# Lo parts that are loaded as weights start 112 bytes into their buffers

## The chip, the cores and the metric

The kernel runs on one core of a Trainium2 chip. TensorE multiplies matrices: an instruction loads a block of weights (128 x 128 here), and a matmul streams up to 512 columns through it into PSUM. VectorE (DVE), ScalarE (ACT) and GpSimd (POOL) do the elementwise work, and SyncE (SP) issues most transfers. The metric is the device time of one execution in microseconds; for the kernel before it is 877.3, the median of three runs.

## The reference

The input x has 2,048 rows of 448 floats. Two layers follow each other, with the same weights. Each is a linear-attention block and a feed-forward block, with a layer norm ahead of each:

```python
phi = lambda t: jnp.where(t > 0, t + 1, jnp.exp(t)) + 1e-6
pq, pk = phi(q), phi(k)                       # q, k, v = x @ wqkv, 16 heads of 28
kv = jnp.einsum("bhsd,bhse->bhde", pk, v)
z = jnp.einsum("bhsd->bhd", pk)
num = jnp.einsum("bhqd,bhde->bhqe", pq, kv)
den = jnp.einsum("bhqd,bhd->bhq", pq, z)[..., None] + 1e-6
o = num / den                                 # then @ wo
...
h = gelu(jnp.einsum("bsd,df->bsf", x, w1) + b1)    # 448 -> 1792
return jnp.einsum("bsf,fd->bsd", h, w2) + b2       # 1792 -> 448
...
x = x + A(layernorm(x)); x = x + B(layernorm(x))   # twice
```

Everything is float32.

## The kernel before

**Split operands.** TensorE takes a rounded float32 (`F32R`) at one column a cycle. To keep accuracy, each operand is split into a hi part, the rounded value, and a lo part, the rest. A product then takes three matmuls: hi by hi, hi by lo, lo by hi. Where only 64 of 448 rows are left over, hi and lo of these rows share one block and two matmuls do.

**Stages.** The 2,048 rows are 16 tiles of 128. For each layer, `phase1` walks over the 16 tiles: the normalized tile is transposed and split into `XH` and `XL`; `stage_k` and `stage_q` multiply it with the weights of k and q (lines 325 to 330, outputs `psk` and `psq`); `stage_g` multiplies the normalized tile itself, as weights, with phi(k) and adds all tiles up into four PSUM banks `G` (lines 526 to 538). `stage_s` makes its hi and lo parts `xnh` and `xnl`. A short stage in an order written out by hand (`ORDER`) then turns G and the weights of v and of the output into one matrix M (`kvp`, line 698, and `mp`, line 708, are plain float32 matmuls there).

Then the feed-forward part goes over four blocks of four tiles and, in each, over 14 steps of 128 of the 1,792 hidden columns. `mlp1` (lines 858 to 862, output `hp`) makes a step's hidden values: 11 matmuls of 512 columns, in which w1 is the weights and the tokens stream. ScalarE applies gelu (line 864) and copies the hi part `gh` (line 867), VectorE subtracts for the lo part `gl` (line 868). `mlp2` (lines 891 to 893, output `y`) has gelu's parts as weights and streams 448 columns of w2: for each of four tiles `gh` by `w2h`, `gh` by `w2l`, `gl` by `w2h`. The loop issues `mlp1` of step i + 1 ahead of `mlp2` of step i, so that gelu of a step has a whole `mlp1` to finish in. In the same steps, after a table of plans, the product of the next block's queries with M is done (`oc_mm`, lines 800 to 804, output `op`, with `qh` and `ql` as weights); for the first block of a layer `o_mm` does it (lines 789 to 791).

**Buffers.** `t512(tag, bufs, name, dt)` takes a tile of 128 x 512 floats, 2,048 bytes a partition, from a ring of `bufs` buffers per tag. The hi parts `xnh`, `gh` and the first block's `qh` use tag A, their lo parts tag B; other queries use E and F. All rings have two buffers here, and all slices that are loaded as weights are 128 columns, 512 bytes, apart. Two unread tiles named `space` (192 and 128 bytes) stand between the others; by the sizes of all tiles in the order of their allocation, the tiles that TensorE reads in its one-pass matmuls begin at multiples of 256 bytes. SBUF is filled nearly to its end.

**Tails.** For the first eight tiles of the first layer the transposition is done on TensorE. The last 64 columns of such a tile are copied twice into a 128 x 128 tile `tail` (line 413, ScalarE), which is transposed like the other three pieces (lines 257 and 264). `tail` has two buffers. `b2b` is the bias b2 on all partitions: one transfer fills it behind `phase1` of the first layer (line 1003), and `add_bias` (line 820) adds it on GpSimd in the feed-forward part.

The tile framework places the semaphores: a reader waits for the writer of what it reads, a writer for the readers of what it overwrites. Instructions run in the order of the program on each engine.

Of the kernel before, what the change touches and what calls it, by code (L numbers as in the profile page):

```python
# [9 lines left out]
F32 = mybir.dt.float32  # L10
F32R = mybir.dt.float32r
# [11 lines left out]
def linear_attn_mlp_kernel(  # L23
# [16 lines left out]
    F = w1.shape[1]  # L40
# [4 lines left out]
    G = 112  # L45
# [6 lines left out]
    work = ctx.enter_context(tc.tile_pool(name="work", bufs=2))  # L52
# [9 lines left out]
    def bank(tag, bufs, name):  # L62
        return psum.tile([128, 512], F32, name=name, tag=tag, bufs=bufs)
# [4 lines left out]
        bufs = NH if tag == "H" else bufs  # L68
        return work.tile([128, D], dt, name=name, tag=tag, bufs=bufs)

    def t512(tag, bufs, name, dt=F32):
        return work.tile([128, 512], dt, name=name, tag=tag, bufs=bufs)

    def f(ap):
        return ap.bitcast(F32)
# [82 lines left out]

    ones = consts.tile([128, 128], F32R, name="ones")
    one = t512("e", 3, "one")[:, :128]  # L160
    dve.memset(one, 1.0)
    dve.tensor_copy(ones, one)
# [23 lines left out]
    b2b = consts.tile([128, D], F32, name="b2b")  # L186
# [123 lines left out]
    def split_t(key, t, hi, lo, eng=dve):  # L310

        x = spreads[key, t // 2].rearrange("p (i c u n) -> p u c i n", i=4, c=4, n=32)[:, t % 2]
        h = hi.rearrange("p (c i n) -> p c i n", c=4, n=32)
        act.copy(h, x)  # L314
        eng.tensor_tensor(lo.rearrange("p (c i n) -> p c i n", c=4, n=32), x, f(h), op=OP.subtract)  # L315
# [85 lines left out]
    tails = {}  # L401
# [4 lines left out]
    def stage_n(l, t):  # L406

        xs, mv, rs = sts.pop((l, t))
        dve.tensor_scalar(xs, xs, mv[:, 0:1], rs, op0=OP.subtract, op1=OP.mult)
        xns[l, t] = xs  # L410
        if t < TURNED[l]:
            d = tails[l, t] = work.tile([128, 128], F32, name="tail", tag="tail", bufs=2)
            act.copy(d.rearrange("p (u n) -> p u n", u=2), xs[:, None, TL:].to_broadcast([128, 2, 64]))

    def stage_t(l, t):
# [24 lines left out]
    def stage_s(l, t):  # L440
        xn = xns.pop((l, t))
        h = t512("A", 2, "xnh", F32R)
        lo = t512("B", 2, "xnl", F32R)
        act.copy(h[:, :D], xn)  # L444
        pool.tensor_tensor(lo[:, :TL], xn[:, :TL], f(h[:, :TL]), op=OP.subtract)  # L445
        pool.tensor_tensor(h[:, D:], xn[:, TL:], f(h[:, TL:D]), op=OP.subtract)
        split[l, t] = (h, lo)
# [139 lines left out]
    def launch(za):  # L587
        for tok in LAUNCH.split():
            name, (j, *c) = tok.rstrip("0123456789"), [int(i) for i in tok if i.isdigit()]
            if name in ("ka", "qa"):  # L590
                split_hi(name[0], j, st_k if name == "ka" else st_q)
            elif name in ("kb", "qb"):
                split_lo(name[0], j, st_k if name == "kb" else st_q, pool if tok in ("kb1", "kb2", "qb0", "qb2") else dve)
            elif name in ("ha", "hb", "la", "lb"):
                split_half(("a", 0, 0), j, "ab".index(name[1]), "hi" if name[0] == "h" else "lo")
            elif name == "T":
                launch_t(j)
            elif name == "K":
                stage_k(0, j, c)
            elif name == "Q":  # L600
                stage_q(0, j, c)
            elif name == "kl":
                stage_kl(0, j, za)
            else:
                {"a": stage_a, "n": stage_n, "kp": stage_kphi, "kh": stage_kh, "s": stage_s}[name](0, j)

    def phase1(l, tr):
# [6 lines left out]
        for t in range(l == 0, NT):  # L614
            norm = NORM[l][t] if t < len(NORM[l]) else ()
            for tok in STEPS.get((l, t), STEP).split():
                if tok[1:].isdigit() and tok[0] in "anv":
                    {"a": stage_a, "n": stage_n, "v": stage_t}[tok[0]](l, int(tok[1:]))
                elif tok == "q1":
                    stage_qphi(1)  # L620
# [9 lines left out]
                elif tok == "n":  # L630
                    for u in norm:
                        stage_n(l, u)
# [109 lines left out]
    pqt, qs, pzs = {}, {}, {}  # L742
# [31 lines left out]
    def q_split(l, b, j):  # L774
        tp = tqs.pop((l, b, j))
        qh = t512("A", 2, "qh", F32R)[:G]
        ql = t512("B", 2, "ql", F32R)[:G]
        act.copy(qh, tp[:G])
        dve.tensor_sub(ql, tp[:G], f(qh))
        qs[l, b, j] = (qh, ql)  # L780
# [55 lines left out]
        turn(pqt.pop((l, b * 4 + j)), ("q", l, b), j)  # L836

    def q_part(l, b, j):
        qs[l, b, j] = t512("E", 2, "qh", F32R), t512("F", 2, "ql", F32R)
        split_t(("q", l, b), j, *qs[l, b, j])  # L840

    def m_prep(l, b, j):
# [9 lines left out]
    def mlp1(l, b, i):  # L852
        hp = bank("h", 2, "hp")
        s = slice(i * 128, (i + 1) * 128)
        x = blocks["m", l, b]
        o = hp.rearrange("p (t n) -> p t n", t=4)
        for c in range(3):
            pe.matmul(o, w1h[:, c, s], x.moving(x.hi, c), start=(c == 0), stop=False)  # L858
            pe.matmul(o, w1l[:, c, s], x.moving(x.hi, c), start=False, stop=False)  # L859
            pe.matmul(o, w1h[:, c, s], x.moving(x.lo, c), start=False, stop=False)  # L860
        pe.matmul(o, w1x[:, s], x.moving(x.hi, 3), start=False, stop=False)  # L861
        pe.matmul(o, w1x[:, s], x.moving(x.lo, 3), start=False, stop=True)  # L862
        g = t512("e", 3, "g")
        act.activation(g, hp, AF.Gelu_apprx_tanh, bias=b1s[:, i:i + 1])  # L864
        gh = t512("A", 2, "gh", F32R)
        gl = t512("B", 2, "gl", F32R)
        act.copy(gh, g)  # L867
        dve.tensor_sub(gl, g, f(gh))  # L868
        gs[i] = (gh, gl)
# [78 lines left out]
    def behind(l, b, i, tr):  # L948
        for tok in (PLAN_0, PLAN_1, PLAN)[min(b, 2)][i].split():
# [6 lines left out]
            if name == "ld":  # L956
                load_pq(l, k, j)
            elif name == "g":
                load_x(l, k * 4 + j)
            elif name == "z":  # L960
                q_z(l, k, j, tr)
            elif name == "p":
                q_prep(l, k, j, tr)
            elif name == "sq":
                store_sq(("q", l, k), j)
            elif name == "lq":
                spread(("q", l, k), j)
            elif name == "q":
                q_part(l, k, j)
            elif name == "o":  # L970
                oc_mm(l, k, j, tr)
                o_ln(l, k, j)
            elif name == "n":
                m_prep(l, k, j)
            elif name == "sx":
                store_sq(("m", l, k), j)
            elif name == "lx":
                spread(("m", l, k), j)
            elif name == "x":
                m_part(l, k, j)  # L980
# [12 lines left out]
    for l in range(LAYERS):  # L993
# [11 lines left out]
        def pre(j):  # L1005
# [9 lines left out]
            kv=lambda j: trans_kv(tr), mask=lambda j: trans_mask(tr), m=lambda j: trans_m(tr, j),  # L1015
            ms=lambda j: trans_ms(tr, j), qz=lambda j: q_z(l, 0, j, tr), qs=lambda j: q_scale(l, 0, j, tr),
            tq=lambda j: q_transpose(l, 0, j), qq=lambda j: q_split(l, 0, j), o=lambda j: o_mm(l, 0, j, tr),
            la=lambda j: o_ln(l, 0, j), lb=lambda j: o_n(l, 0, j), T=lambda j: m_transpose(l, 0, j),
            x=lambda j: m_split(l, 0, j), tu=lambda j: turn(xns.pop(("m", l, j)), ("m", l, 0), j),
            st=lambda j: store_sq(("m", l, 0), 0), sp=lambda j: spread(("m", l, 0), 0), pre=pre, b=biases)  # L1020
        for tok in ORDER.split():
            name, j = tok.rstrip("0123456789"), int("0" + tok.lstrip("abcdefghijklmnopqrstuvwxyzQTG"))
            getattr(tok_, name)(j)
        assert not fill and not qo
        table(AF.Gelu_apprx_tanh)
        q_z(l, 1, 0, tr)
        mlp1(l, 0, 0)
        trans_chunks(tr)
        for b in range(NB):
# [6 lines left out]
            for i in range(NF):  # L1036
                if i + 1 < NF:
                    mlp1(l, b, i + 1)
                elif nxt:
                    mlp1(l, b + 1, 0)  # L1040
                if l == 0 and b == 0 and i:
                    background(1, 1)
                if i == NF - 2 and not nxt and l + 1 < LAYERS:
                    table(AF.Exp)
                if 9 <= i < 13:
                    add_bias(l, b, i - 9)
                if nxt:
                    behind(l, b, i, tr)
                elif l + 1 < LAYERS:
                    if i == 2:  # L1050
                        split_kq("k", st_k)
                    if i == 5:
                        split_kq("q", st_q)
                    if i in (3, 4, 6, 7, 8):
                        t = (3, 4, 6, 7, 8).index(i)
                        stage_a(l + 1, t)
                        stage_n(l + 1, t)
                        stage_t(l + 1, t)
                        if t % 2:
                            stage_sp(l + 1, t)  # L1060
                    if 9 <= i < 13:
                        stage_x(l + 1, i - 9)
                mlp2(l, b, i, acc)
# [28 lines left out]
```

## Time and profile before

| | |
|---|---|
| median of three runs | 877.3 us (876.67 to 877.49) |
| span of the profiled execution, first to last instruction | 875.2 us |
| TensorE busy with matmuls | 870.1 us, 4182 records |
| weight loads busy | 772.0 us, 4182 records |
| VectorE, ScalarE, GpSimd busy | 491.2, 344.4, 221.1 us |
| matmuls y, three groups of 447 | 365 ns each by the record |
| matmuls hp, 512 columns | about 391 ns each by the record |

How to read it: a matmul's record lasts longer than the distance to the next one's start, because they are pipelined, and so the durations of matmuls overlap and their ends are modelled. PE is the row of matmuls, PEld that of the weight loads that run beside them. For the profiled execution the trace has the span; the time of the runs holds what lies around it as well. In the timeline a row is start, duration, engine, line, operation, output and inputs, and shapes, all times in us. In a group's row the numbers behind the bar are the busy time in us, the mean of one in ns, and the engine's idle time ahead of it with what ended it.

### The profile page before, as it was taken

The page shows a single profiled execution, that of the slowest core. Times are in us where ns is not written, and L with a number is a line of the kernel's source. Part 1 is how long each engine was busy: PE and PEld are TensorE (multiplying, and loading weights), DVE is VectorE, ACT ScalarE, POOL GpSimd, SP SyncE. Part 2 cuts the span into 40 slices and gives each one's busy share as a digit, 9 for nine tenths or more (in the row PEclk, how much of TensorE's full clock was granted, in tenths as well). Part 3 has the DMA queues.
Part 4 walks back from the last instruction along what each step waited for, and adds up shares of the span by engine and source line. Part 5 has one row for each costly group of instructions (what it writes and reads, how often), then busy time and mean ns, then how long its engine had stood idle before and what let it go on. Part 6 is the DMA issues. An engine that isn't in the chain of part 4 may idle for free.

```text
span 875.2 us, 11679 instructions
## 1 busy us (share of the span) xinstructions
PE 870.1 (99%) x4182; PEld 772.0 (88%) x4182; DVE 491.2 (56%) x958; ACT 344.4 (39%) x606; POOL 221.1 (25%) x250
## 2 busy tenths in 40 slices
PE   9999999999999999999999999999999999999998
PEld 8999988888888888888899998888888888888887
DVE  7878586658455443226477876864674483433112
ACT  6776635324323322333356665332233133223221
POOL 5566532235013112012222344110220140140000
PEclk9999999999999999999999999999999999999999
DMA  5474637633313402051145543352332423111001
GB/s 160 136 239 152 207 88 210 184 93 125 133 60 105 156 0 97 1 179 49 48 141 188 166 128 106 104 182 80 110 109 91 134 71 115 49 49 43 0 1 43
DMA packets 63642, 94.76 MB, mean 108 GB/s; under 512 B 8928, under 2 KB 58720, under 8 KB 63584
## 3 DMA queue, kind: packets, MB, share of 16 engines
q1 hardware_dynamic: 63408, 93.87, 33.5%
q8 instruction: 33, 0.54, 0.3%
q14 instruction: 25, 0.20, 0.1%
q10 hardware_dynamic: 176, 0.14, 0.0%
HBM read 56.17 MB, written 34.60 MB: 104 GB/s over the span
## 4 chain that ended last, share of the span: by engine, by line
PE 98%; DVE 0%; DMA 0%; POOL 0%; issue 0%; DVEq 0%; POOLq 0%
PE y L893 10%; PE y L892 10%; PE y L891 10%; PE hp L859 9%; PE hp L860 9%; PE hp L858 9%; PE hp L861 3%; PE hp L862 3%; PE psk L326 2%; PE psq L325 2%; PE psq L327 2%; PE psq L326 2%; PE psk L327 2%; PE psk L325 2%; PE G L534 2%; PE G L535 2%
## 5 line engine op out<-in xcount | busy, mean ns | idle before, releaser
L868 DVE TENSOR_TENSOR gl<-g,gh 128x512 fp32r<-128x512 f32 x112 | 82.6, 737 | 300.0 <-ACT gh L867 300.0
L864 ACT ACTIVATE g<-hp,b1s 128x512 f32<-128x512 f32 x112 | 77.1, 688 | 406.6 <-PE hp L862 401.8
L893 PE MATMUL y<-w2h,gl 128*128 128x448 f32 x447 | 163.3, 365 | 0.0
L892 PE MATMUL y<-w2l,gh 128*128 128x448 f32 x447 | 163.3, 365 | 0.0
L891 PE MATMUL y<-w2h,gh 128*128 128x448 f32 x447 | 163.3, 365 | 0.0
L859 PE MATMUL hp<-XH,w1l 128*128 128x512 f32 x336 | 131.5, 392 | 0.0
L858 PE MATMUL hp<-XH,w1h 128*128 128x512 f32 x336 | 131.2, 391 | 0.0
L860 PE MATMUL hp<-XL,w1h 128*128 128x512 f32 x336 | 131.2, 391 | 0.0
L214 POOL TENSOR_TENSOR brs<-bve,mhalf 128x1 f32<-128x1 f32 x64 | 39.4, 616 | 283.9 <-DVE bve L212 280.8
L891 PEld LDWEIGHTS y<-w2h,gh 128*128 128x128 f32 x447 | 84.0, 188 | 9.0
L892 PEld LDWEIGHTS y<-w2l,gh 128*128 128x128 f32 x447 | 84.0, 188 | 8.3
L893 PEld LDWEIGHTS y<-w2h,gl 128*128 128x128 f32 x447 | 84.0, 188 | 6.6
L860 PEld LDWEIGHTS hp<-XL,w1h 128*128 128x128 f32 x336 | 63.1, 188 | 14.1 <-issue 0.6
L859 PEld LDWEIGHTS hp<-XH,w1l 128*128 128x128 f32 x336 | 63.1, 188 | 11.3
L858 PEld LDWEIGHTS hp<-XH,w1h 128*128 128x128 f32 x336 | 63.1, 188 | 10.8
L867 ACT CAST gh<-g 128x512 fp32r<-128x512 f32 x112 | 69.7, 622 | 3.6
L751 POOL TENSOR_TENSOR pz<-pq,zb 128x448 f32<-128x448 f32 x32 | 36.6, 1147 | 82.6 <-DVE dn L757 65.9
L445 POOL TENSOR_TENSOR xnl<-x,xnh 128x384 fp32r<-128x384 f32 x32 | 35.0, 1092 | 72.6 <-ACT xnh L444 40.6
L315 DVE TENSOR_TENSOR XL<-sp,XH 128x512 fp32r<-128x512 f32 x50 | 44.4, 893 | 4.1 <-ACT XH L314 4.1
L862 PE MATMUL hp<-XL,w1x 128*128 128x512 f32 x112 | 43.6, 389 | 0.0
L861 PE MATMUL hp<-XH,w1x 128*128 128x512 f32 x112 | 43.6, 389 | 0.0
L820 POOL TENSOR_TENSOR x<-x,b2b 128x448 f32<-128x448 f32 x32 | 42.0, 1332 | 0.0
(169 smaller groups left out, 1566.8 us busy)
## 6 DMA issues: line engine op xcount, KB each, us to landing
x<-in_A_x_dram SPq DMA_DIRECT2D x32, 224.0 KB, 3.9
pq_d<-eq SPq DMA_DIRECT2D x32, 224.0 KB, 2.8
pq<-pq_d SPq DMA_DIRECT2D x32, 224.0 KB, 3.2
sq_m<-sq SPq DMA_DIRECT2D x14, 512.0 KB, 2.8
sp<-sq_m SPq DMA_DIRECT2D x56, 128.0 KB, 2.9
x<-x_d SPq DMA_DIRECT2D x32, 224.0 KB, 3.2
sq_a<-sq SPq DMA_DIRECT2D x12, 512.0 KB, 2.9
sp<-sq_a SPq DMA_DIRECT2D x48, 128.0 KB, 2.9
```

Of the source, the lines that this page charges most:

```text
L315: eng.tensor_tensor(lo.rearrange("p (c i n) -> p c i n", c=4, n=32), x, f(h), op=OP.subtract)
L858: pe.matmul(o, w1h[:, c, s], x.moving(x.hi, c), start=(c == 0), stop=False)
L859: pe.matmul(o, w1l[:, c, s], x.moving(x.hi, c), start=False, stop=False)
L860: pe.matmul(o, w1h[:, c, s], x.moving(x.lo, c), start=False, stop=False)
L861: pe.matmul(o, w1x[:, s], x.moving(x.hi, 3), start=False, stop=False)
L862: pe.matmul(o, w1x[:, s], x.moving(x.lo, 3), start=False, stop=True)
L864: act.activation(g, hp, AF.Gelu_apprx_tanh, bias=b1s[:, i:i + 1])
L867: act.copy(gh, g)
L868: dve.tensor_sub(gl, g, f(gh))
L891: pe.matmul(acc[j], gh[:, s], w2h[:, i], start=first, stop=False)
L892: pe.matmul(acc[j], gh[:, s], w2l[:, i], start=False, stop=False)
L893: pe.matmul(acc[j], gl[:, s], w2h[:, i], start=False, stop=stop)
```

## The change

Buffers of tags B and F become 576 floats long, 2,304 bytes, and `t512` gets a parameter `at`: the tile that it returns is the 512 floats from there. The lo parts that are loaded as weights (`xnl`, `ql` in both forms, `gl`) are taken at 28 floats, 112 bytes. Hi parts and all other tiles of these tags (`kl`, `zl`, `Ml`, `gt`) stay at 0. To make room for the four longer buffers (4 x 256 bytes), the two `tail` tiles (2 x 512 bytes) go: tails take turns in the first two 128-column parts of `b2b`, ahead of its transfer.

```diff
-    def t512(tag, bufs, name, dt=F32):
-        return work.tile([128, 512], dt, name=name, tag=tag, bufs=bufs)
+    APART = 28
+
+    def t512(tag, bufs, name, dt=F32, at=0):
+        n = 576 if tag in "BF" else 512
+        return work.tile([128, n], dt, name=name, tag=tag, bufs=bufs)[:, at:at + 512]
...
         if t < TURNED[l]:
-            d = tails[l, t] = work.tile([128, 128], F32, name="tail", tag="tail", bufs=2)
+            d = tails[l, t] = b2b[:, t % 2 * 128:][:, :128]
...
         h = t512("A", 2, "xnh", F32R)
-        lo = t512("B", 2, "xnl", F32R)
+        lo = t512("B", 2, "xnl", F32R, APART)
...
         qh = t512("A", 2, "qh", F32R)[:G]
-        ql = t512("B", 2, "ql", F32R)[:G]
+        ql = t512("B", 2, "ql", F32R, APART)[:G]
...
-        qs[l, b, j] = t512("E", 2, "qh", F32R), t512("F", 2, "ql", F32R)
+        qs[l, b, j] = t512("E", 2, "qh", F32R), t512("F", 2, "ql", F32R, APART)
...
         gh = t512("A", 2, "gh", F32R)
-        gl = t512("B", 2, "gl", F32R)
+        gl = t512("B", 2, "gl", F32R, APART)
```

## The prediction

> **What bounds the kernel.** I read the page first: the span, the busy shares, the granted clock and the chain.
>
> ```profile
> span 875.2 us, 11679 instructions
> PE 870.1 (99%) x4182; PEld 772.0 (88%) x4182; DVE 491.2 (56%) x958; ACT 344.4 (39%) x606; POOL 221.1 (25%) x250
> ...
> PEclk9999999999999999999999999999999999999999
> ...
> PE 98%; DVE 0%; DMA 0%; POOL 0%; issue 0%; DVEq 0%; POOLq 0%
> ```
>
> TensorE has work for 870.1 of 875.2 us at full granted clock, and the chain that ended last is 98% TensorE. So no other engine's work matters unless it makes TensorE wait, and the time is a count of matmuls times the distance from one start to the next. A busy share cannot show that distance, because matmuls overlap. I take it from the timeline of starts, in one step of the feed-forward part and in one stretch of the attention part of the first layer:
>
> ```profile
> 599.87 0.37 PE L891 MATMUL y<-w2h,gh 128*128 128x448 f32 x1
> ...
> 602.30 0.39 PE L858 MATMUL hp<-XH,w1h 128*128 128x512 f32 x1
> ...
> 603.00 0.40 PE L858 MATMUL hp<-XH,w1h 128*128 128x512 f32 x1
> ...
> 603.69 0.39 PE L858 MATMUL hp<-XH,w1h 128*128 128x512 f32 x1
> ...
> 604.82 0.36 PE L800 MATMUL op<-wq,qh 128*128 128x448 f32 x1
> ```
>
> ```profile
> 98.63 0.37 PE L534 MATMUL G<-kh,xnh 128*128 128x448 f32 x1
> ...
> 100.90 0.37 PE L325 MATMUL psq<-wq,XH 128*128 128x448 f32 x1
> ```
>
> ```profile
> 506.27 0.36 PE L534 MATMUL G<-kh,xnh 128*128 128x448 f32 x1
> ...
> 508.50 0.36 PE L325 MATMUL psk<-wk,XH 128*128 128x448 f32 x1
> ```
>
> Twelve y matmuls take 602.30 - 599.87 = 2.43 us, 202.5 ns each. Eleven G matmuls take 2.23 us late (202.7 ns each) and 2.27 us early (206.4 ns each): the same work, the same weights and columns, at two paces. With 512 columns, the first three behind y take 0.70 us (233 ns each) and the last five 1.13 us (226 ns each). So the distance has a part that depends on what came just before, not on the operation alone.
>
> What would the columns alone take? Two groups in plain float32 help, in which a record streams its columns twice:
>
> ```profile
> 108.19 3.31 PE L698 MATMUL kvp<-gt,stg 128*112 128x112 f32 x32
> 111.33 0.60 PE L769 MATMUL tq<-ident,pq 128*112 128x128 f32 x4
> ...
> 114.46 2.80 PE L708 MATMUL mp<-wot,kvm 112*112 112x448 f32 x7
> ...
> L708 PE MATMUL mp<-wot,kvm x16: 537/539/541, 114.5 to 546.9; 112*112 112x448 f32 x16
> ```
>
> The seven mp records last 2.80 us, the last one 0.54, so six distances make 2.26 us, 377 ns for two passes of 448 columns, 188 ns a pass, although each record has its own weight load. kvp gives (111.33 - 108.19) / 32 = 98 ns for two passes of 112, 49 ns a pass. Against 188 ns, a one-pass 448-column matmul loses 202.5 - 188 = 14.5 ns beside its weight load. (That a record is two passes I infer from these times.) This loss of about 14 ns, and its swing of 4 ns between the two paces, is all that a change of addresses can touch.
>
> **The change, part by part.** No instruction, semaphore or DMA is added or removed. Four things move.
>
> (1) The lo tiles used as weights begin 112 bytes into a longer buffer. The groups that load them:
>
> ```profile
> L893 PEld LDWEIGHTS y<-w2h,gl x447: 187/188/188, 143.3 to 870.4; 128*128 128x128 f32 x149
> ...
> L536 PEld LDWEIGHTS G<-kh,xnl x90: 187/188/189, 18.1 to 535.0; 128*128 128x128 f32 x90
> ...
> L528 PEld LDWEIGHTS G<-kh,xnl x6: 188/188/188, 94.7 to 525.1; 128*128 128x128 f32 x6
> ...
> L802 PEld LDWEIGHTS op<-wq,ql x72: 187/188/188, 168.0 to 762.0; 128*128 128x128 f32 x72
> L791 PEld LDWEIGHTS op<-Mh,ql x32: 187/188/188, 118.1 to 559.8; 112*128 112x128 f32 x32
> ...
> L804 PEld LDWEIGHTS op<-wq,ql x24: 187/188/188, 169.6 to 762.4; 128*128 128x128 f32 x24
> ```
>
> 447 + 90 + 6 + 72 + 32 + 24 = 671 loads (two more in the last output tile). Each takes 188 ns and runs under the matmul before it, and each is one of a group of about three 448-column matmuls, hi, hi, lo. What does the new start cost? By the sizes of the tiles in the order they are allocated, and with the program's unread spacers, every operand of these matmuls begins at a multiple of 256 bytes, so the trace holds no such start. The nearest rows are kvp and mp above: their weights are slices 448 bytes apart, thus at odd multiples of 64 bytes too, and each keeps one pace. But those have slack, 112 is no multiple of 64, and the one-pass matmuls have none. So the price is bounded from both sides:
> - Gain at most the whole loss of the lo matmul: 671 x 14.5 ns = 9.7 us.
> - Gain if the 448-column distance loses as little as the settled 512-column one: 226 ns less 64 columns at 188 / 448 = 0.42 ns is 199 ns. Single distances that short occur beside longer ones (rows below: 0.21, then 0.19), so 202.5 is the mean of a walk. Only the lo distance to 199: 671 x 3.5 ns = 2.3 us. All three of a group: 7.0 us.
> - Loss if all three lock at the 206.4 ns of the early G: 671 x 3 x 3.9 ns = 7.9 us; the lo distance alone: 2.6 us.
>
> ```profile
> 606.64 0.36 PE L803 MATMUL op<-wq,qh 128*128 128x448 f32 x1
> 606.85 0.36 PE L804 MATMUL op<-wq,ql 128*128 128x448 f32 x1
> 607.04 0.37 PE L891 MATMUL y<-w2h,gh 128*128 128x448 f32 x1
> ```
>
> I take the middle of the two middle gains, 7 ns a group, 671 x 7 ns = 4.7 us. A load whose reads no longer run in step with those of the columns is what the shift makes; the walk has room to 199 below and the shift breaks a regularity that all loads share. The sign rests on weak ground, and I say so in the chances. In sentences of its own: the Trainium skill, page "TensorE: Matmul & The Clock Gate", section "Step-by-step: what each phase is for", has two independent SBUF read ports on TensorE, so that "Loading the next tile's weights doesn't steal SBUF read bandwidth from the running matmul". By that rule the sum of this part is 0 and the time 877.3. That section does not explain the 14.5 ns here, which vanish where columns stream at half the rate; that is what speaks against it.
>
> (2) The writers of these tiles write at the new start. Their time has cover:
>
> ```profile
> 300.93 0.69 DVE L868 TENSOR_TENSOR gl<-g,gh 128x512 fp32r<-128x512 f32 x1 [2.12 <-ACT gh L867]
> ...
> 304.50 0.19 PEld L893 LDWEIGHTS y<-w2h,gl 128*128 128x128 f32 x1
> ...
> L868 DVE TENSOR_TENSOR gl<-g,gh 128x512 fp32r<-128x512 f32 x112 | 82.6, 737 | 300.0 <-ACT gh L867 300.0
> ```
>
> gl is done at 301.62 and first loaded at 304.50, 2.9 us later. Even twice the 737 ns would fit; without that cover it would be 112 x 0.7 = 78 us. VectorE idles 300 us before this line, so what stands behind it on its queue moves little. xnl and ql are written the same way. Price 0.
>
> (3) The tails of the first eight tiles are written into the first 256 columns of b2b, which is idle then:
>
> ```profile
> L413 ACT COPY tail<-x x8: 289/298/299, 6.6 to 41.1; 128x128 f32<-128x128 f32 x8
> L257 PEld LDWEIGHTS tp<-ident,tail x6: 139/140/142, 17.7 to 51.3; 128*128 128x128 f32 x6
> ...
> PE tp L264 <- ACT tail L413: 0.2, 1, 0.2
> ...
> L1003 SPq DMA_DIRECT2D b2b<-in_B_b_dram x1: 1588/1588/1588, 112.3 to 112.3; - x1
> ```
>
> Two halves take turns as two buffers did. The last read is at 51.3, the load of b2b at 112.3, so its new wait behind the reads costs SP's queue nothing. Were each copy to wait for the other half's reader, ACT would be held and TensorE would pay about one copy each, 8 x 0.3 = 2.4 us at most; the only wait of TensorE on a tail today is 0.2 us. Price 0.
>
> (4) Tiles behind move by whole multiples of 256 bytes. Every 1,792-byte row of w2h that streams today already differs in such multiples, at one pace. Price 0.
>
> The profiled execution has a span of 875.2; the median of the runs, 877.3, lies 2.1 above it, start and end around the span. Sum: 875.2 - 4.7 = 870.5 of span, **872.6 us** of time.
>
> **Rivals.**
> - The start makes no difference, because the reads of weights and of columns do not meet at all: 877.3, within 875.5 to 879.1. The rule of the page above is this case. For it: y, G and op, with operands at many multiples of 256, share 202.5 ns to a few tenths. Against it: all those starts are alike below 256 bytes.
> - It goes up: a load that starts inside a 64-byte stretch touches one more of them than an aligned one, comes in later against the columns, and the group falls into the slow pace. Place: y, G and op. Price: 2.6 us (lo alone) to 7.9 (all three), so 879.9 to 885.2, taken at 881.5. It decides once the mean of the 2,013 matmuls rises by 0.9 ns (1.75 us). For it: the early G shows that this pace holds for long stretches once entered. Against it: there it follows a break of the stream, and y has none.
> - The tails serialise the start: 877.3 + 2.4 = 879.7 at most; the order of steps writes each tail after the transposes of the one two before, so this is unlikely.
>
> **How the numbers follow.** A measurement of this kernel can tell about 0.2% (1.75 us) from no change; the three runs spread by 0.8 us. Faster as summed 0.50, with a range of its own from 868 to 875; no difference 0.17; the slow pace 0.30; the tails 0.03. That makes faster 0.50, same 0.17, slower 0.33. The range for 8 in 10 goes from 868.0, a little above the bound of the whole loss (877.3 - 9.7 = 867.6), to 882.5, past the middle of the slow case; it leaves out some 5 in 100 below and 10 to 15 above.
>
> **What would show it.** In the changed kernel's timeline, twelve y matmuls (four groups) in 2.40 us (2.42 if only the lo distance moves, 2.39 if all three do), and G and op alike, with K and Q, whose weights stay, at 202.7: the sum is right. 2.43 with all stretches as before: the start does not matter. 2.48: the slow pace. LDWEIGHTS of gl longer than 188 ns would show a load that itself got longer. A wait of TensorE on tail over 0.2 us, or of L413 on TensorE, would show (3) wrong; a wait of PEld on gl, (2). The prediction is wrong at its root if the gain or loss lies in groups without a lo load.

## The result and the profile after

The changed kernel takes 870.83 us (870.49 to 871.35) against 876.98 (876.64 to 877.49). The ratio is 0.9927, with a 95% interval from 0.9913 to 0.9941: 6.15 us less. From its page, the lines that answer to those shown of before (the code below line 71 stands three lines lower):

```profile
span 869.0 us, 11679 instructions
...
PE 863.5 (99%) x4182; PEld 771.0 (89%) x4182; DVE 491.6 (57%) x958; ACT 344.7 (40%) x606; POOL 221.5 (25%) x250
...
PEclk9999999999999999999999999999999999999999
...
PE 98%; DMA 0%; DVE 0%; ACT 0%; POOL 0%; issue 0%; SPq 0%; DVEq 0%; ACTq 0%
...
L895 PE MATMUL y<-w2l,gh 128*128 128x448 f32 x447 | 163.6, 366 | 0.0
L894 PE MATMUL y<-w2h,gh 128*128 128x448 f32 x447 | 162.0, 362 | 0.0
L896 PE MATMUL y<-w2h,gl 128*128 128x448 f32 x447 | 160.0, 358 | 0.0
...
L862 PE MATMUL hp<-XH,w1l 128*128 128x512 f32 x336 | 130.7, 389 | 0.0
```

Nothing is less work: 4182 matmuls, the same clock, TensorE still 98% of the chain. The records of the three y lines, 365 ns each before, are now 362, 366 and 358. How the distances changed is seen in the timeline, here one step of y, the settled and the first hp behind it:

```profile
350.41 0.36 PE L894 MATMUL y<-w2h,gh 128*128 128x448 f32 x1
350.61 0.37 PE L895 MATMUL y<-w2l,gh 128*128 128x448 f32 x1
350.82 0.36 PE L896 MATMUL y<-w2h,gl 128*128 128x448 f32 x1
351.01 0.36 PE L894 MATMUL y<-w2h,gh 128*128 128x448 f32 x1
...
352.81 0.39 PE L861 MATMUL hp<-XH,w1h 128*128 128x512 f32 x1
...
353.49 0.39 PE L861 MATMUL hp<-XH,w1h 128*128 128x512 f32 x1
```

Twelve y matmuls take 352.81 - 350.41 = 2.40 us instead of 2.43. A group of three is 0.20, 0.21, 0.19: in the trace's full resolution the steps of 199, 205 and 196 ns repeat to the end of the step, 200.0 on average, where before a walk of 199, 207, 202, 203, 202 gave 202.6. A stream whose distances repeat in this way is called settled below, and their average is its pace. And the first three hp behind y take 0.68 us (227 ns each) where they took 0.70 (233).

Summed over the trace, from each matmul's start to the next, by what it computes (448 and 512 columns; us):

| | before | changed | difference |
|---|---|---|---|
| y | 271.87 | 268.36 | -3.51 |
| hp | 281.45 | 279.64 | -1.81 |
| queries by M (op) | 73.25 | 72.61 | -0.64 |
| G | 72.22 | 71.95 | -0.27 |
| K and Q | 144.29 | 144.35 | +0.06 |
| everything else | 27.19 | 27.11 | -0.08 |
| sum | 870.27 | 864.02 | -6.25 |

By the last row but one of the table, TensorE spends as long on all other work, waits included, as before. The weight loads themselves have not changed:

```profile
L896 PEld LDWEIGHTS y<-w2h,gl x447: 187/188/188, 143.0 to 864.2; 128*128 128x128 f32 x149
L896 PE MATMUL y<-w2h,gl x447: 358/358/358, 143.2 to 864.4; 128*128 128x448 f32 x149
```

G shows that a shifted start does not by itself give the good pace. One stretch of the changed kernel:

```profile
503.01 0.36 PE L537 MATMUL G<-kh,xnh 128*128 128x448 f32 x1
503.22 0.37 PE L538 MATMUL G<-kl,xnh 128*128 128x448 f32 x1
503.42 0.36 PE L539 MATMUL G<-kh,xnl 128*128 128x448 f32 x1
...
504.24 0.36 PE L537 MATMUL G<-kh,xnh 128*128 128x448 f32 x1
```

Six G matmuls take 1.23 us, 205 ns each, with the lo part shifted, more than the 202.7 of before; other stretches of G end at 200. The average gains little.

### The profile page after: what moved, and what is told of

Its sections match the earlier page's. It is cut to its first block, busy times and chain, and to the rows that moved or that the text cites. A ratio compares the mean times of both kernels' runs of the same rounds, so it can differ in the third digit from the quotient of the medians.

```text
span 869.0 us, 11679 instructions
## 1 busy us (share of the span) xinstructions
PE 863.5 (99%) x4182; PEld 771.0 (89%) x4182; DVE 491.6 (57%) x958; ACT 344.7 (40%) x606; POOL 221.5 (25%) x250
## 4 chain that ended last, share of the span: by engine, by line
PE 98%; DMA 0%; DVE 0%; ACT 0%; POOL 0%; issue 0%; SPq 0%; DVEq 0%; ACTq 0%
PE y L895 10%; PE y L894 10%; PE y L896 10%; PE hp L863 9%; PE hp L861 9%; PE hp L862 9%; PE hp L865 3%; PE hp L864 3%; PE psk L329 2%; PE psq L329 2%; PE psq L328 2%; PE psq L330 2%; PE psk L330 2%; PE psk L328 2%; PE G L538 2%; PE G L537 2%
## 5 line engine op out<-in xcount | busy, mean ns | idle before, releaser
L896 PE MATMUL y<-w2h,gl 128*128 128x448 f32 x447 | 160.0, 358 | 0.0
```

Source lines behind the costliest of these rows:

```text
L896: pe.matmul(acc[j], gl[:, s], w2h[:, i], start=False, stop=stop)
```

## The experiments

The theory of the prediction (S): the start of the lo load changes how it meets the other reads, and so the pace of a hi, hi, lo stream. Rivals: the layout or the tails do it (L); hi and lo loads have to start apart from each other (P); a load has to start apart from the streamed columns (C); the start in SBUF itself counts (D). Where an edit makes the start depend on the step, one trace holds a whole series.

**The layout alone.** Diffs are against the changed kernel.

```diff
-    APART = 28
+    APART = 0
```

> The changed kernel with all lo parts back at offset 0; the longer buffers and the tails in b2b stay. Theory A (the start address of the lo loads is the whole effect): twelve y matmuls in 2.43 us again, the first hp matmuls behind y slow again (0.70 us for three), time 877 +- 0.5. Rival L (the moved buffers or the tails give the gain): time stays near 871 and y near 2.40.

Measured: 877.26 us, ratio to before 0.9999 (0.9988 to 1.001). In its timeline y and hp are back where they were:

```profile
338.21 0.36 PE L894 MATMUL y<-w2h,gh 128*128 128x448 f32 x1
...
340.64 0.39 PE L861 MATMUL hp<-XH,w1h 128*128 128x512 f32 x1
...
341.33 0.39 PE L861 MATMUL hp<-XH,w1h 128*128 128x512 f32 x1
```

2.43 us for twelve y, 0.69 for three hp. So the longer buffers, the moved tiles and the tails in b2b cost and bring nothing that can be measured; the start addresses are the whole effect. L falls.

**Which start.** Three kernels shift the loads of y by 16 bytes a hidden step, a fourth the streamed rows of w2:

```diff
-        gl = t512("B", 2, "gl", F32R, APART)
+        gl = t512("B", 2, "gl", F32R, 4 * i)
```

> gl of hidden step i starts at 16 x i bytes (i = 0 to 13), one look. Theory R (what counts is where a load starts against the other loads or the columns, with some period): step 0 takes 2.43 us for its twelve y matmuls, step 7 (112 bytes) 2.40, and the others differ among each other, with a period of 64 or 128 bytes. Theory M (any start off the common multiple will do): all steps but 0 (and perhaps 4, 8, 12, the multiples of 64 bytes) take 2.40. Time between 870.8 and 877.

```diff
-        n = 576 if tag in "BF" else 512
+        n = 576 if tag in "AB" else 512
...
-        qs[l, b, j] = t512("E", 2, "qh", F32R), t512("F", 2, "ql", F32R, APART)
+        qs[l, b, j] = t512("E", 2, "qh", F32R), t512("F", 2, "ql", F32R)
...
-        gh = t512("A", 2, "gh", F32R)
-        gl = t512("B", 2, "gl", F32R, APART)
+        gh = t512("A", 2, "gh", F32R, 4 * i)
+        gl = t512("B", 2, "gl", F32R, 4 * i)
```

> gh and gl of step i both start at 16 x i bytes; tags A and B have the longer buffers, the other queries' ql is back at 0. Theory P (hi and lo loads must start apart from each other): all steps take 2.43 us as before, since consecutive loads start alike. Theory C (a load must start apart from the columns that stream): step 0 takes 2.43, step 7 takes 2.40 or less, since all three loads of a group are now apart from the columns of w2. Time near 877 under P, below 874 under C.

The third is the second with `gl` at 0.

> gh of step i starts at 16 x i bytes and gl at 0. Theory P (apart from each other): the mirror of the sweep of gl, step 7 or the one at the opposite distance (16 bytes, step 1) near 2.40 us, with the short and the long distance at the hi loads. Theory C (apart from the columns): two of three loads moved, so steps that gain in the sweep of gl gain about twice as much here, 2.37. Step 0 takes 2.43 under both.

The fourth has `APART = 0`, buffers of 512 floats, and rows of w2 that are 452 floats apart:

```diff
-    w2h = wts.tile([128, NF, D], F32R, name="w2h")
-    w2l = wts.tile([128, NF, D], F32R, name="w2l")
+    w2h = wts.tile([128, NF, D + 4], F32R, name="w2h")
+    wts.tile([128, 8], F32, name="space1")
+    w2l = wts.tile([128, NF, D + 4], F32R, name="w2l")
+    wts.tile([128, 8], F32, name="space2")
```

> The streamed side alone: row i of w2h and w2l starts 16 x i bytes past a multiple of 256 (i = 0 to 13), gh and gl at 0, one look. Theory C: the steps differ among each other as in the sweep of gh and gl together, with the sign of the shift turned (2.43 at 0, up to 2.466, at the best 2.40). Rival D: all steps take 2.43 us.

Each of these four kernels was executed once: lo alone took 875.42 us, hi alone 876.63, hi and lo 877.58, the columns 879.53. Twelve y matmuls, from the first one's start to the start of the next hp, where hp stands on both sides (us; the executions of one step agree within 0.002):

| start, bytes | lo | hi | hi and lo | columns of w2 |
|---|---|---|---|---|
| 0 | 2.43 | 2.43 | 2.43 | 2.43 |
| 16 | 2.40 | 2.41 | 2.46 | 2.44 |
| 32 | 2.43 | 2.43 | 2.43 | 2.48 |
| 48 | 2.44 | 2.45 | 2.44 | 2.44 |
| 64 | 2.44 | 2.42 | 2.43 | 2.41 |
| 80 | 2.43 | 2.42 | 2.44 | 2.44 |
| 96 | 2.44 | 2.40 | 2.47 | 2.46 |
| 112 | 2.40 | 2.45 | 2.45 | 2.47 |
| 128 | 2.43 | 2.46 | 2.45 | 2.45 |
| 144 | 2.43 | 2.43 | 2.43 | 2.48 |
| 160 | 2.44 | 2.45 | 2.47 | 2.43 |
| 176 | 2.43 | 2.44 | 2.44 | 2.45 |
| 192 | 2.43 | 2.41 | 2.40 | 2.42 |
| 208 | 2.40 | 2.42 | 2.45 | 2.44 |

Two steps of the first of these kernels, with gl at 112 and at 48 bytes, in its timeline:

```profile
342.29 0.36 PE L894 MATMUL y<-w2h,gh 128*128 128x448 f32 x1
...
344.69 0.39 PE L861 MATMUL hp<-XH,w1h 128*128 128x512 f32 x1
...
391.47 0.36 PE L894 MATMUL y<-w2h,gh 128*128 128x448 f32 x1
...
393.91 0.39 PE L861 MATMUL hp<-XH,w1h 128*128 128x512 f32 x1
```

2.40 and 2.44. What follows: (1) Starts matter in steps of 16 bytes, on both sides, the loads' and the columns'. (2) Few starts are good. Of the 13 shifted starts of lo, three gain 0.03 us a step, six gain 0.006, and four lose up to 0.01. Over all 14 starts y sums to 271.45 us, against 271.90 with `APART = 0` and 268.36 at 112 bytes, so an average start gains an eighth of what 112 does. Shifts of hi and lo together, or of the columns, mostly cost. (3) The best in each series with shifted loads is 2.40, 200 ns a matmul; none is below. (4) For lo alone it comes at 16, 112 and 208 bytes, 96 apart; the other series show no such simple period.

Of the theories, M (any start off the multiple will do) and the period of 64 or 128 bytes in R fall with the first series. P falls: hi and lo both at 192 bytes, alike, give 2.40, and hi at 112 with lo at 0 gives 2.45. C missed its numbers too: hi and lo at 112 take 2.45, not 2.40, and no step of the hi series comes near 2.37. Its mirror holds in part. If distances repeat after 256 bytes, which no run tests, columns at s should do what hi and lo do at 256 - s: eight of the eleven pairs agree within 0.011 us in the traces, three (columns at 112, 144 and 160) differ by 0.032 to 0.043. D in its plain form, by which the columns' start changes nothing, falls with the last series.

The table holds only behind hp. With hi and lo at 96 bytes, the same step of the same kernel runs at two paces:

```profile
177.42 0.36 PE L894 MATMUL y<-w2h,gh 128*128 128x448 f32 x1
...
179.82 0.40 PE L861 MATMUL hp<-XH,w1h 128*128 128x512 f32 x1
...
338.28 0.36 PE L894 MATMUL y<-w2h,gh 128*128 128x448 f32 x1
...
340.75 0.39 PE L861 MATMUL hp<-XH,w1h 128*128 128x512 f32 x1
```

Behind op it takes 2.40 us, with every distance at 200 ns; behind hp it takes 2.47, with 207, 206 and 207 repeating. All eight executions of the step follow this: two stand behind op, six behind hp. So addresses do not fix the pace alone; what ran just before chooses between the two.

**Another good start for all lo parts.** `APART = 4`.

> All shifted lo parts at 16 bytes in place of 112. From the sweep of gl (2.400 us at 16 and at 112): y and hp as at 112, so 870.8 within 0.7; G and op may differ, by less than 0.7 us. A theory in which 112 bytes is special would have about 877.

Measured, in two runs: 870.63 us, ratio 0.9927 (0.9907 to 0.9947). y sums to 268.38 us as at 112 bytes, G to 71.66 and op to 72.96. The number 112 is not special.

**Distance or place.** Three kernels, executed once each (881.07, 876.38 and 878.78 us), are read by their y steps. In the first, all operands of y stand 96 bytes on; in the next two lo is apart from hi by 112, with the columns shifted as well and without.

```diff
-    APART = 28
+    APART = 0
...
-        n = 576 if tag in "BF" else 512
+        n = 512
...
+    wts.tile([128, 24], F32, name="space1")
     w2h = wts.tile([128, NF, D], F32R, name="w2h")
     w2l = wts.tile([128, NF, D], F32R, name="w2l")
+    wts.tile([128, 40], F32, name="space2")
...
+        if (l, t) == (0, 0):
+            work.tile([128, 24], F32, name="space", tag="space1", bufs=1)
         h = t512("A", 2, "xnh", F32R)
         lo = t512("B", 2, "xnl", F32R, APART)
+        if (l, t) == (0, 0):
+            work.tile([128, 40], F32, name="space", tag="space2", bufs=1)
```

The unread tiles of 24 floats move what is laid out behind them by 96 bytes, those of 40 bring the rest back to a multiple of 256.

> gh, gl, w2h and w2l all start 96 bytes past a multiple of 256, one look (xnh, xnl and the first block's queries move with gh and gl; no lo part stands apart). With gh and gl alone at 96 bytes twelve y matmuls took 2.465 us. Theory C (what counts is the distance between loaded weights and streamed columns): back to 2.433 us, as with all at 0. Rival D (the start of the loads in SBUF itself counts, wherever the columns are): 2.465 us.

It took 2.478 us: neither theory's number. The distances are those of before, and the pace is the 206.7 ns that the early G of before settled at, also with every operand at 0. Behind op, instead of behind hp, the same step takes 2.438, and there the walk of before (199, 207, 202, 203, 202) is back. So equal starts have two paces, and what came before picks one; this run does not separate C from D. In the same kernel both loads of G start at 96 bytes and its columns at 0: most stretches of G settle at 200 ns, and it sums to 71.32 us, less than in the changed kernel (71.95).

The second keeps `APART` for B alone (other queries at 0), with the same four spacers:

> gh, w2h and w2l at 96 bytes past a multiple of 256, gl at 208, so that within y all distances are those of the changed kernel; other queries' ql back at 0. Theory C (distances between loads and columns set the pace): twelve y matmuls in 2.40 us. Rival D (the start in SBUF itself): anything else, above 2.42.

The third is the second without the two spacers around w2:

> The control of the run before: gh at 96 bytes and gl at 208 as there, w2h and w2l back at 0. Theory C: the distance of the loads to the columns is now another one, so another pace than 2.40 us. Theory P (hi and lo apart by 112 is enough): 2.40 here too.

From the timeline of the second, with loads and columns all 96 bytes on:

```profile
338.24 0.37 PE L900 MATMUL y<-w2h,gh 128*128 128x448 f32 x1
...
338.65 0.36 PE L902 MATMUL y<-w2h,gl 128*128 128x448 f32 x1
...
340.45 0.36 PE L902 MATMUL y<-w2h,gl 128*128 128x448 f32 x1
340.65 0.39 PE L867 MATMUL hp<-XH,w1h 128*128 128x512 f32 x1
```

From the third matmul to the last, nine distances take 1.80 us, 200 ns each, with 196, 199, 205 repeating as in the changed kernel; only the two distances at the entry (208, 204 ns) and the last (204) are long, where hp, still at 0, meets a y at 96. The whole step is 2.416 us, between the two forecasts. In the third kernel, with the same loads but columns at 0, the step is 2.429 and no stretch settles at 200 (202, 200, 207, 207, 197, 203). So P falls again, and moving loads and columns together keeps the pattern of distances, while moving the loads alone does not: that speaks for C, as far as one shift tells. It does not decide the pace alone: at equal starts, and with hi and lo at 96, the same distances gave two paces, by what came before.

**More loads of the same kind.** XL, the lo half of the transposed tokens, is loaded in K and Q, but streams in hp.

```diff
-            self.lo = work.tile([128, 2048], F32R, name="XL", tag="XL", bufs=2)
+            k = len(blocks) % 2
+            at = (4, 20)[k]
+            self.lo = work.tile([128, 2048 + at], F32R, name="XL", tag=f"XL{k}", bufs=1)[:, at:]
...
-        rd = work.tile([128, H], F32, name="rd", tag="rd", bufs=2)
+        rd = work.tile([128, H], F32, name="rd", tag="rd", bufs=1)
```

The single buffer of `rd`, a small tile that VectorE writes and reads in the attention part, makes room for the longer XL.

> The changed kernel, and in addition the lo halves XL of the transposed blocks start 16 bytes (one buffer) and 112 bytes (the other) into theirs, the two starts at which gl took 2.40 us for twelve; they are weights in K and Q (256 of 704 loads there) and stream in hp. Theory S (the start of every third load decides the pace of a hi, hi, lo stream): eleven K or Q matmuls go from 2.23 us to about 2.20, and G, which follows in the same stream, from a mix of 200 and 204 ns to 200: 704 x 2.65 ns + 352 x 2 ns = 2.6 us, so about 868.3. Rival: only y and op have a state to gain from, K, Q and G keep their pace, 870.8; or hp, whose streamed XL now starts elsewhere, loses its 226.7 ns, and the time is above 871.

Measured: 879.75 us, ratio to before 1.0025 (1.0013 to 1.0038). The rival about hp was right. From its timeline:

```profile
341.70 0.39 PE L866 MATMUL hp<-XH,w1h 128*128 128x512 f32 x1
...
343.78 0.40 PE L869 MATMUL hp<-XH,w1x 128*128 128x512 f32 x1
...
344.25 0.37 PE L899 MATMUL y<-w2h,gh 128*128 128x448 f32 x1
```

Eleven hp, of which four stream XL, take 2.55 us, 232 ns each, not 227: hp sums to 285.75 us, 6.1 more than in the changed kernel, of which 0.56 is one longer wait for XL and the rest is pace. K, Q and G together gain 0.69 us. And y, whose addresses are untouched, is entered differently: 2.40 us in some of its steps, 2.45 in others, 2.85 us more in all, and op adds another 0.99.

So XL of the K and Q blocks alone was shifted, by 16 bytes (`Block(4 if key[0] == "a" else 0)`, with room made by the single `rd` as before and by tags B0 and B1, in which lo stands at 16 and at 112):

> The changed kernel, in addition XL of the blocks that are weights in K and Q starts 16 bytes into its buffer, XL of the blocks that stream in hp stays at 0; gl, xnl and the first block's ql start at 16 or 112 bytes by the buffer. From the run with all XL moved: K, Q and G together 0.7 us less than in the changed kernel, while hp and y keep its 226.7 and 200 ns: 870.1 +- 0.6, better than the changed kernel by less than 0.2%. If moving XL as such disturbs y: above 871.5.

Measured: 871.89 us, ratio to before 0.9942 (0.9929 to 0.9956), so not better than the changed kernel. By its trace the paces came out as meant: K, Q and G together take 1.31 us less, y and hp settle at 200.0 and 226.7 ns. But hp sums to 0.98 us more and op to 0.61, and these are waits. The first rows are of this kernel, at the start of the feed-forward part, the second of the changed one:

```profile
137.39 0.40 PE L877 MATMUL hp<-XH,w1l 128*128 128x512 f32 x1
138.17 0.47 PE L878 MATMUL hp<-XL,w1h 128*128 128x512 f32 x1 [0.39 <-DVE XL L288]
...
137.35 0.68 DVE L288 TENSOR_TENSOR XL<-tp,XH 128x512 fp32r<-128x512 f32 x1
```

```profile
137.85 0.40 PE L862 MATMUL hp<-XH,w1l 128*128 128x512 f32 x1
138.14 0.47 PE L863 MATMUL hp<-XL,w1h 128*128 128x512 f32 x1
...
137.31 0.68 DVE L273 TENSOR_TENSOR XL<-tp,XH 128x512 fp32r<-128x512 f32 x1
```

TensorE arrives 0.46 us earlier, VectorE writes the last part of XL at the same time, and the distance to the third hp is 0.78 instead of 0.29 us, once in each layer: 0.98 us in all. In op, two loads of `ql` wait for VectorE likewise and cost about 0.54 of its 0.61. Why `ql` comes later was not separated (the second buffer of `rd` is gone as well).

**Is the rest paid per loaded column?** The remaining loss, 200 less 188 ns, with fewer columns in the loads:

```diff
-            pe.matmul(acc[j], gh[:, s], w2h[:, i], start=first, stop=False)
-            pe.matmul(acc[j], gh[:, s], w2l[:, i], start=False, stop=False)
-            pe.matmul(acc[j], gl[:, s], w2h[:, i], start=False, stop=stop)
+            n = {2: 96, 3: 96, 5: 64, 6: 64, 8: 32, 9: 32}.get(i, 128)
+            s = slice(j * 128, j * 128 + n)
+            pe.matmul(acc[j][:n], gh[:, s], w2h[:, i], start=first, stop=False)
+            pe.matmul(acc[j][:n], gh[:, s], w2l[:, i], start=False, stop=False)
+            pe.matmul(acc[j][:n], gl[:, s], w2h[:, i], start=False, stop=stop)
```

> The changed kernel, in which y of hidden steps 2 and 3 loads and computes 96 of the 128 rows of each token tile, of steps 5 and 6 64, of 8 and 9 32 (the rows left out do not get these steps' part). Streamed columns stay 448. Theory W (what a one-pass matmul loses beside its columns, 200 less 188 = 12 ns, is paid per loaded weight column): twelve y matmuls take 2.40 us at 128, about 2.36 at 96, 2.33 at 64, 2.29 at 32. Rival F (a fixed price of changing weights): 2.40 at all.

The kernel took 873.16 us in its one run. Groups of its loads, and one step with 32 columns:

```profile
L896 PEld LDWEIGHTS y<-w2h,gh 128*128 128x128 f32 x255 | 47.7, 187 | 5.5
...
L896 PEld LDWEIGHTS y<-w2h,gh 128*32 128x32 f32 x64 | 6.9, 108 | 5.2
```

```profile
346.18 0.36 PE L896 MATMUL y<-w2h,gh 128*32 128x448 f32 x1
...
348.61 0.40 PE L861 MATMUL hp<-XH,w1h 128*128 128x512 f32 x1
```

A load of 32 columns takes 108 ns instead of 187, but twelve y take 2.43 us, not the 2.29 of theory W, and more than the 2.40 at 128; 64 columns give 2.43 to 2.45, 96 give 2.44 to 2.46. W falls, and F with its 2.40 at all widths does not come out as stated either. A fixed price, with a pace that each pattern of reads disturbs otherwise, would fit. The settled paces of the changed kernel agree with it: 226.7 ns for 512 columns and 200.0 for 448 differ by 0.417 ns a column, which makes 186.7 ns for 448 columns and leaves 13.3 ns beside the columns at both widths (an estimate from two paces). What the price is stays open.

In the Trainium skill, page "TensorE: Matmul & The Clock Gate", section "Back-to-back issue gap", the formula for an isolated matmul at the full clock gives an estimate of 448 / 2.4 + 2.5 = 189 ns for 448 columns; no one-pass stream here settled below 200. The two independent read ports of the same page of the Trainium skill, section "Step-by-step: what each phase is for", agree with a loss that does not shrink with the load; they leave unexplained that the starts of loads and columns matter at all.

## Why the prediction was right

- **The sum.** Forecast 872.6, measured 870.8, inside the likeliest case's own range. Gain forecast 4.7 us, measured 6.15: the term of part 1 came out near its size, and a term that the sum did not have came on top.
- **Part 1, the pace.** Said: 7 ns a group, 2.40 us for twelve y. Measured: 2.40, and y, G and op together -4.42 us for 671 groups, 6.6 ns a group. It is uneven: y gives 3.51 / 447 = 7.9 ns, op and G 0.91 / 224 = 4.1. The bound of 199 ns, taken from hp less 64 columns, came out: the settled pace is 200.0. That the middle between two bounds came so near is luck, since no row gave the 7 ns. The shape was not foreseen: the lo matmul does not become short by itself. Within y, the distance while gl is being loaded grew (202.8 to 205.0 ns), the one after gl starts to multiply shrank (201.8 to 195.9), and the third fell from 202.7 to 199.5. The prediction took its 188 ns for the columns alone from plain float rows, and so its remark that those rows lose nothing was true by construction; the two settled paces now give 186.7 without them.
- **The term that was missing.** hp gives 1.81 us, and it has no shifted load. The slow first three hp (0.70 us) stood in the prediction's own rows, but were put into no term: the text treated the price as one of the three matmuls of a group and let the stream behind it stand. Behind the y of the changed kernel hp starts settled, at 227 ns. Why is open: with y settled at the same 200 ns but 96 bytes on, hp starts slow and sums to 282.15 us. The text had said that it would be wrong at its root if the gain lay in groups without a lo load; 29% of it did, and still by the same cause, since all of it goes with `APART = 0`.
- **Why the sign was right.** The reason given, that reads which run in step are pulled out of step, is not shown. By the sweep, breaking the alignment is not enough: of the 13 shifted starts of lo, three give 2.40, the others 2.43 to 2.44, against 2.43 at 0. That 112 bytes is one of the three was luck as far as the prediction goes, which had no row to choose it by. A chance of one half for this side was as much as that argument carried.
- **The rivals.** That the start makes no difference falls with the run at 0 against the changed kernel, 877.26 and 870.83. **The slow pace** did not come in y, but it exists at other starts (2.48 at columns shifted by 32), and G has stretches at 204 ns, between the two paces of before. The stretch of 64 bytes that this rival named is shown by no run: lo at 64, 128 and 192 bytes gives 2.44, 2.43 and 2.43. **The tails** cost nothing that can be measured: 877.26 with them in b2b. Their one wait of TensorE is 0.4 us in the changed kernel, over the 0.2 that the prediction set as a sign; the total does not show it.
- **Writers, queues, moved tiles.** Price 0 as forecast. The run at 0 carries the moved tiles and the queues; the writers at 112 bytes take 743 ns for gl in the changed kernel, 737 before, and TensorE has no wait for it.

## What to carry to other kernels

Where TensorE is 99% busy, look at distances between starts, not at records: a pace that walks, or that differs for the same work in two places, is time that addresses may give back. Try starts in 16-byte steps of loads and of streamed columns apart, in one kernel with one start per loop step, and read the whole series from one trace; but read each start behind the same neighbour that it will have. Judge a shift by the whole time, since the stream behind it is entered in another state: moving XL gained 0.7 us where it was meant to and lost 10 elsewhere. And look for new waits: where TensorE became 0.46 us earlier than VectorE, the gain was lost there.

## What was not expected of the hardware

- Starts of operands move a steady stream of one-pass matmuls between 200.0 and 206.7 ns for 448 columns, 3%, at unchanged loads (188 ns), clock and work.
- The same addresses have more than one lasting pace: y with hi and lo at 96 bytes runs at 200 ns a matmul behind op and at 206.7 behind hp; y at 112 bytes runs 2.40 or 2.45 us in the run with XL moved; G with all operands at 0 ran at 202.6 and 206.7 in the kernel before.
- Shifting XL, which four of eleven hp matmuls stream, by 16 or 112 bytes costs 4.5 ns of 227 a matmul on average, 5.5 us in all.
- Loads of a quarter of the columns are 79 ns shorter and the stream is not faster.
